# Linear attention and a GELU network on one core: a new load order and finer pieces for the first batch

## The chip, the cores and the metric

The kernel runs on one core of one Trainium2 chip. A time is the device time of one execution in microseconds. The span is what the hardware profiler shows of one execution, from the first instruction to the last; the profiled execution has a time of its own, which is a little longer than its span. All moments named below are counted from the start of the span.

## The reference

There are 8 batches, 8 heads, 576 tokens and 64 features per head. Each batch goes through a linear attention with cosine weights, and the result through a two-layer network with d_model 512 and d_ff 2048.

```python
theta = pi / 2 * pos / S                     # pos = 0 .. 575
phi(x) = concat(max(x, 0) * cos(theta), max(x, 0) * sin(theta))     # 64 -> 128 features
kv  = sum over tokens of phi(k)[f] * v[d]    # 128 x 64 for each head
z   = sum over tokens of phi(k)              # 128 for each head
att = (phi(q) @ kv) / (phi(q) . z + 1e-6)
x   = att, heads side by side                # 4608 x 512
h   = x @ w_in                               # 512 -> 2048
out = (h * sigmoid(1.702 * h)) @ w_out       # 2048 -> 512
```

Inputs and output are float32; the kernel computes its products in bfloat16 with float32 sums.

## The kernel before

One batch, 576 tokens, is one block. For each block the kernel does the following.

- `trig` (L134) and `trig_q` (L143) build phi(k) and phi(q) from the float32 tiles `kf` and `qf`. One call makes two instructions, cosine and sine. In batch 0 the nine strips j of 64 tokens are spread over VectorE and ScalarE (`act=True`).
- `kv_mm` (L197) sums phi(k) against v on TensorE, and against ones for z. `kv_evac` (L205) copies the result from PSUM to `kvs` on VectorE.
- phi(q) is turned so that features lie on partitions, in `qT`. In batch 0 TensorE does this (`qturn_pe`, L166) and VectorE or ScalarE copies it out (`qevac`, L173). In later batches SP issues transposes by DMA (`qturn_dma`, L182).
- `num_mm` (L211) multiplies 128 tokens of `qT` with `kvs`. `num_div` (L219) divides by the last column in three VectorE instructions. Its result `xn` is turned by TensorE (`xturn_mm`, L236) and copied to `x` by ScalarE (`xturn_evac`, L243) in batches 0 and 1, and by DMA (`xturn_dma`) later. Accumulators of `kv_mm`, `num_mm` and `xturn_mm` come from a PSUM pool `pat` of two buffers.
- `mm1_part` (L260) multiplies x with 128 columns of w_in, four products over the 512 features; a group `fc` is one such set of 128 hidden features, and there are 16. `gelu` (L267) applies the activation on ScalarE. The last 64 tokens of a batch go through `mm1_tail` (L278), in two halves of eight groups, with products of 64 columns (L284).
- `mm2` (L300) multiplies the activated groups with w_out for 128 tokens t at a time, in pieces lo to hi of the 16 groups. ScalarE copies the sum to `ysb`, and Pool stores it. Accumulators of `mm1`, `mm2`, `qturn_pe` and the warm-up `idle` (L314) share the PSUM pool `pmm` of four buffers.

The order of the instructions on every engine is the order in which the code is written (`tc.manual_schedule()`). Nothing is moved by a planner.

The loads go through two queues. SP issues k and q of batch 0 in two pieces each (L62, L63). Pool issues v of batch 0 into `vb` as bfloat16, w_in and w_out (cast to bfloat16 on the way), and the loads of later batches. Two of Pool's instructions are there only to make it wait: a copy of one element of `kf` into `gate` (L124), and one of `vb` (L129):

```python
nc.gpsimd.tensor_copy(gate[0:1, 0:1], kf[0:1, 0, 0:1])
for i in (0, 2):
    nc.gpsimd.dma_start(out=vb[:, i:i + 2], in_=src_of(v, 0, i, i + 2))
load_win(0, 512)
load_win(512, 1024)
nc.gpsimd.tensor_copy(gate[0:1, 1:2], vb[0:1, 3, 0:1])
load_win(1024, 1536)
load_win(1536, 2048)
```

TensorE starts with products of zeros (`idle`, L354 and L355) until phi(k) is there. `start_block` (L325) opens a batch whose x is made on TensorE: it multiplies the first four groups 128 tokens at a time, with the later numerators and turns of x between them, and then one whole group of 512 tokens. For batch 0 it runs over groups 0 to 3 and then 4; groups 5 to 15 follow whole. While batch 0 is in mm2, the kv sum and the first numerators of batch 1 are computed between its pieces, and so are the first two turns of x (L434 to L444, `opened=True`). From batch 1 on, the loop at L447 computes, during mm1 of batch b, phi(q), phi(k) and v of batch b + 1 on VectorE, and at group 15 its kv sum on TensorE. A third copy by Pool (L415) holds the loads of batch 2 until the transposes of batch 1's q have landed.

Of the kernel before, what the change touches and what calls it, by code (L numbers as in the profile page):

```python
# [9 lines left out]
F32 = mybir.dt.float32  # L10
# [9 lines left out]
def kernel(  # L20
# [9 lines left out]
    nc = tc.nc  # L30
# [21 lines left out]
    def raw(name, dt=F32):  # L52
        return one.tile([128, NI, S], dt, name=name)

    def src_of(src, b, i0=0, i1=NI):
        return src[b, 2 * i0:2 * i1].rearrange("(i hh) (p j) d -> (hh p) i (j d)", hh=2, j=NS)

    qf = one.tile([128, 2560], F32, name="qf")
    kf, vf, vb = raw("kf"), raw("vf"), raw("vb", BF16)
    qf0 = qf[:, 0:NI * S].rearrange("p (i e) -> p i e", i=NI)  # L60
    for t, src, cut in ((kf, k, 192), (qf0, q, 256)):
        nc.sync.dma_start(out=t[:, :, 0:cut], in_=src_of(src, 0)[:, :, 0:cut])  # L62
        nc.sync.dma_start(out=t[:, :, cut:S], in_=src_of(src, 0)[:, :, cut:S])  # L63


    NP = NS + 5
# [1 line left out]
    nc.gpsimd.iota(pos_i[:, 0:NS], pattern=[[1, NS]], base=0, channel_multiplier=NS)  # L68
    nc.gpsimd.iota(pos_i[:, NS:NS + 4], pattern=[[1, 4]], base=0, channel_multiplier=4)
    nc.gpsimd.iota(pos_i[:, NS + 4:NP], pattern=[[1, 1]], base=512, channel_multiplier=1)  # L70
    ident = const.tile([128, 128], BF16)
    nc.gpsimd.memset(ident, 1.0)
    nc.gpsimd.affine_select(out=ident, in_=ident, compare_op=mybir.AluOpType.is_equal,
# [22 lines left out]
    qn0 = qn.rearrange("p c h f -> p (c h f)")[:, 0:NS * NI * 128].rearrange(  # L96
        "p (j i f) -> p j i f", j=NS, i=NI)
    qT = one.tile([128, H, 640], BF16, name="qT")
    w_in_sb = one.tile([128, KC, d_ff], BF16, name="w_in_sb")
    w_out_sb = one.tile([128, FC, d_model], BF16, name="w_out_sb")  # L100
    nc.gpsimd.memset(vt[:, :, :, 64:66], 1.0)
    nc.gpsimd.memset(qT[:, :, S:640], 0.0)


    win_r = moe_w_in.rearrange("(kc p) f -> p kc f", p=128)
    wout_r = moe_w_out.rearrange("(fc p) d -> p fc d", p=128)

    def load(t, src, b):
        nc.gpsimd.dma_start(out=t, in_=src_of(src, b))
# [4 lines left out]
        nc.gpsimd.dma_start(out=qf[0:64, 2048:2560].rearrange("p (h e) -> p h e", h=H),  # L114
                            in_=q[b, :, 512:S, :].rearrange("h p d -> p h d"))

    def load_win(f0, f1):
        nc.gpsimd.dma_start(out=w_in_sb[:, :, f0:f1], in_=win_r[:, :, f0:f1])

    def load_wout(g):  # L120
        nc.gpsimd.dma_start(out=w_out_sb[:, ts(g, 4), :], in_=wout_r[:, ts(g, 4), :])

    gate = const.tile([1, 4], F32)
    nc.gpsimd.tensor_copy(gate[0:1, 0:1], kf[0:1, 0, 0:1])  # L124
    for i in (0, 2):
        nc.gpsimd.dma_start(out=vb[:, i:i + 2], in_=src_of(v, 0, i, i + 2))
    load_win(0, 512)
    load_win(512, 1024)
    nc.gpsimd.tensor_copy(gate[0:1, 1:2], vb[0:1, 3, 0:1])  # L129
    load_win(1024, 1536)  # L130
    load_win(1536, 2048)


    def trig(dst, src, j, act=False):  # L134
# [70 lines left out]
    def kv_evac(i0, i1):  # L205
        o = st["kvs"][:, :, i0:i1, 0:65]
        nc.vector.tensor_copy(o, st["ps", i0].rearrange("p hh (i e) -> p hh i e", e=65))  # L207
# [28 lines left out]
    def xturn_mm(c):  # L236
        ps, xn = nums[c]
        xv = xn.rearrange("p a h e -> p (a h e)")
        for kc in range(KC):
            o = ps[:, kc // 2, ds(264 + (kc % 2) * 64, 64)].bitcast(BF16)  # L240
            nc.tensor.transpose(o, xv[:, ts(kc, 128)], ident)  # L241

    def xturn_evac(b, c):  # L243
        ps = nums.pop(c)[0]
        n = 128 if c < 4 else 64
        i = ps[:, :, 264:392].bitcast(BF16).rearrange("p a (k t) -> p a k t", k=2)[:, :, :, 0:n]
        o = x[b][:, :, c * 128:c * 128 + n].rearrange("p (a k) t -> p a k t", a=2)
        nc.scalar.activation(o, i, AF.Copy)
# [11 lines left out]
    def mm1_part(b, fc, t0, t1):  # L260
        if t0 == 0:
            hp[fc] = pmm.tile([128, MT], F32, name="mm")
        for kc in range(KC):
            nc.tensor.matmul(hp[fc][:, t0:t1], w_in_sb[:, kc, ts(fc, 128)], x[b][:, kc, t0:t1],  # L264
                             start=(kc == 0), stop=(kc == KC - 1))

    def gelu(fc):  # L267
        g = gpool.tile([128, MT], BF16, name="g")
        nc.scalar.activation(g, hp.pop(fc), AF.Gelu_apprx_sigmoid)  # L269
        gT[fc] = g  # L270

    def mm1(b, fc):
        mm1_part(b, fc, 0, MT)
# [4 lines left out]
    def mm1_tail(b, half):  # L278
        if half == 0 and b % 2 == 0:
            gt[0] = gpool.tile([128, FC, 128], BF16, name="gtail", bufs=2)  # L280
        hps = pmm.tile([128, 8, 64], F32, name="mm")
        for f in range(8):
            for kc in range(KC):
                nc.tensor.matmul(hps[:, f], w_in_sb[:, kc, ts(half * 8 + f, 128)], x[b][:, kc, MT:S],  # L284
                                 start=(kc == 0), stop=(kc == KC - 1))
        nc.scalar.activation(gt[0][:, ts(half, 8), ts(b % 2, 64)], hps, AF.Gelu_apprx_sigmoid)  # L286

# [29 lines left out]
            nc.tensor.matmul(w[:, 0:cols], warm[:, 0:128], warm[:, 0:cols], start=True, stop=True)  # L317

    def vb_rhs(r, i, j):
        return vb[r, i, ts(j, 64)]  # L320

    def vt_rhs(r, i, j):
        return vt[r, j, i, 0:65]

    def start_block(b, opened=False):  # L325

        if not opened:
            xturn_mm(0)
            xturn_evac(b, 0)
            xturn_mm(1)  # L330
            xturn_evac(b, 1)
            num_mm(2)
            num_div(2)
        for c in range(4):
            for fc in range(4):
                mm1_part(b, fc, c * 128, c * 128 + 128)
            if c == 0:
                num_mm(3)
                num_div(3)
                xturn_mm(2)  # L340
                xturn_evac(b, 2)
            if c == 1:
                num_mm(4)
                num_div(4)
                xturn_mm(3)
                xturn_evac(b, 3)
        for fc in range(4):
            gelu(fc)
        mm1(b, 4)
        xturn_mm(4)  # L350
        xturn_evac(b, 4)


    idle(12)  # L354
    idle(100, 64)  # L355
    for j in (0, 1):
        trig(kr, kf, j)
    for j in (2, 6, 7, 8):
        trig(kr, kf, j, act=True)
    for j in (3, 4, 5):  # L360
        trig(kr, kf, j)
    kv_open(0, 2)
    kv_open(2, 4)
    kv_mm(0, NI, lambda r, i, j: ones[r, 0:1], 64, 1)
    for j in (0, 1):
        trig(qn0, qf0, j)
    qturn_pe(0)
    for j in (2, 3):
        trig(qn0, qf0, j, act=True)
    qturn_pe(1)  # L370
    idle(3)
    for j in (4, 5):
        trig(qn0, qf0, j)
    qturn_pe(2)
    for j in (6, 7):
        trig(qn0, qf0, j, act=True)
    qevac(0)
    trig(qn0, qf0, 8)
    qevac(1, act=True)
    qevac(2, act=True)  # L380
    kv_mm(0, 2, vb_rhs, 0, 64)
    kv_evac(0, 2)
    kv_mm(2, 4, vb_rhs, 0, 64)
    kv_evac(2, 4)
    qturn_pe(3)
    qevac(3, act=True)
    num_mm(0)
    num_div(0)
    num_mm(1)
    num_div(1)  # L390
    qturn_pe(4)
    qevac(4)
    x_open(0)
    start_block(0)


    load(kf, k, 1)
# [5 lines left out]
    load_wout(3)  # L403
    for j in range(NS):
        trig(kr, kf, j)
    for fc in range(5, FC):
        mm1(0, fc)
    mm1_tail(0, 0)
    mm1_tail(0, 1)
# [9 lines left out]
    for g in range(2):  # L419
        for t in range(4):  # L420
            mm2(0, t, 4 * g, 4 * g + 4)
    mm2(0, 0, 8, 12)
    mm2(0, 1, 8, 12)
    kv_open()
    kv_mm(0, 4, vt_rhs, 0, 65)
    kv_evac(0, 4)
    mm2(0, 2, 8, 12)
    mm2(0, 3, 8, 12)
    num_mm(0)
    num_div(0)  # L430
    num_mm(1)
    num_div(1)
    x_open(1)
    mm2(0, 0, 12, 16)  # L434
    mm2(0, 1, 12, 16)
    xturn_mm(0)
    xturn_evac(1, 0)
    mm2(0, 2, 12, 16)
    xturn_mm(1)
    xturn_evac(1, 1)  # L440
    num_mm(2)
    num_div(2)
    mm2(0, 3, 12, 16)
    start_block(1, opened=True)  # L444


    for b in range(1, B):  # L447
# [73 lines left out]
```

## Time and profile before

| what | value |
|---|---|
| timed runs | 295.7, 301.29, 302.06 us; median 301.29 |
| profiled execution | 295.57 us, span 293.9 us, TensorE clock 0.998 |
| TensorE busy | 283.1 us, 96% of the span |
| VectorE, ScalarE, Pool busy | 123.8, 128.0, 81.9 us |
| products with w_in (L264) | 593 seen, 113.6 us |
| products with w_out (L305) | 509 and 60 seen, 116.0 and 13.6 us |
| tail products with w_in (L284) | 512, 16.2 us |
| loads of batch 0, issue to landing | k 3.3 and 4.9, q 5.7 and 7.3, v 6.4 and 7.0 us |

A group row of the profile gives the line, the engine and the operation, the tiles it writes and reads with their shapes, how often it ran, busy time and mean duration in nanoseconds, and last the idle time of its engine just ahead of it with what ended it. In a timeline row the first two numbers are the start and the length; the brackets hold the idle time before it and what it waited for. In a row of windows there stand the window, its length, then busy time and count for TensorE's products, TensorE's weight loads, VectorE, ScalarE and Pool, the clock granted to TensorE, the share of the DMA engines and GB/s. A product's own duration contains the time through the array; in a stream the distance of the starts is what counts.

### The profile page before, as it was taken

The page shows a single profiled execution, that of the slowest core. Times are in us where ns is not written, and L with a number is a line of the kernel's source. Part 1 is how long each engine was busy: PE and PEld are TensorE (multiplying, and loading weights), DVE is VectorE, ACT ScalarE, POOL GpSimd, SP SyncE. Part 2 cuts the span into 40 slices and gives each one's busy share as a digit, 9 for nine tenths or more (in the row PEclk, how much of TensorE's full clock was granted, in tenths as well). Part 3 has the DMA queues.
Part 4 walks back from the last instruction along what each step waited for, and adds up shares of the span by engine and source line. Part 5 has one row for each costly group of instructions (what it writes and reads, how often), then busy time and mean ns, then how long its engine had stood idle before and what let it go on. Part 6 is the DMA issues. An engine that isn't in the chain of part 4 may idle for free.

```text
span 293.9 us, 6796 instructions
## 1 busy us (share of the span) xinstructions
PE 283.1 (96%) x2832; PEld 155.7 (53%) x2871; DVE 123.8 (42%) x355; ACT 128.0 (44%) x220; POOL 81.9 (28%) x96
## 2 busy tenths in 40 slices
PE   8879999999999999999999999999999999999993
PEld 4775546746544465446454465446454465445443
DVE  4674513791369125930269115950159304200000
ACT  7847642674115721465114641265114651166121
POOL 6361002635216501470215601290114300100111
PEclk9999999999999999999999999999999999999999
DMA  7999997999999876779249983889258402400112
GB/s 254 239 219 276 351 180 109 326 312 228 323 272 184 240 294 142 156 192 365 71 128 171 221 333 96 151 193 386 85 140 153 93 2 75 115 36 0 38 71 73
DMA packets 64238, 53.59 MB, mean 182 GB/s; under 512 B 49552, under 2 KB 56336, under 8 KB 64208
## 3 DMA queue, kind: packets, MB, share of 16 engines
q0 software_dynamic: 13792, 38.87, 43.3%
q1 hardware_dynamic: 50416, 14.30, 28.4%
q8 instruction: 22, 0.36, 0.5%
q14 instruction: 8, 0.07, 0.1%
HBM read 36.70 MB, written 9.44 MB: 157 GB/s over the span
## 4 chain that ended last, share of the span: by engine, by line
PE 95%; issue 1%; DVE 1%; ACT 1%; ACTq 0%
PE mm L305 42%; PE mm L264 37%; PE mm L284 5%; PE at L202 4%; PE at L215 3%; PE mm L317 3%; PE at L241 1%; DVE xn L227 1%; PE mm L170 1%; ACT g L269 1%; DVE inv L225 0%; DVE den L223 0%; ACT ysb L309 0%; DVE warm L76 0%; ACTq L269 0%
## 5 line engine op out<-in xcount | busy, mean ns | idle before, releaser
L305 PE MATMUL mm<-w_out_sb,g 128*128 128x512 bf16 (+1 forms) x509 | 116.0, 372 | 1.1 <-issue 0.2
L264 PE MATMUL mm<-xT,w_in_sb 128*128 128x512 bf16 (+1 forms) x593 | 113.6, 345 | 0.8
L312 POOL DMA_DIRECT2D out_dram<-ysb x44 | 50.7, 1152 | 169.7 <-ACT ysb L309 162.9
L269 ACT ACTIVATE g<-mm 128x512 bf16<-128x512 f32 x128 | 75.6, 598 | 39.6 <-PE mm L264 39.6
L264 PEld LDWEIGHTS <-w_in_sb 128*128 128x128 bf16 x608 | 53.8, 98 | 55.2
L305 PEld LDWEIGHTS <-g 128*128 128x128 bf16 x528 | 49.0, 98 | 50.2
L309 ACT ACTIVATE ysb<-mm 128x512 f32<-128x512 f32 (+1 forms) x37 | 21.7, 586 | 108.1 <-PE mm L305 101.9
L223 DVE TENSOR_SCALAR den<-at 128x8 f32<-128x8 f32 x40 | 6.6, 166 | 60.6 <-PE at L215 60.6
L227 DVE TENSOR_TENSOR xn<-at,inv 128x512 bf16<-128x512 f32 x40 | 27.7, 691 | 2.4 <-DMA xT<-xn 1.0
L207 DVE CAST kvs<-at 128x520 bf16<-128x520 f32 (+1 forms) x9 | 5.8, 642 | 51.3 <-PE at L202 51.2
L141 DVE TENSOR_SCALAR kr<-kf,cosw 128x256 bf16<-128x256 f32 x68 | 23.8, 350 | 6.9 <-DMA kf<-in_k_dram 6.9
L141 DVE TENSOR_SCALAR kr<-kf,sinw 128x256 bf16<-128x256 f32 x68 | 23.1, 340 | 0.0
L215 PEld LDWEIGHTS <-qT 128*128 128x128 bf16 x320 | 14.5, 97 | 7.3
L154 DVE TENSOR_SCALAR qn<-qf,cosw 128x512 bf16<-128x512 f32 (+1 forms) x33 | 15.8, 478 | 3.9 <-DMA qf<-in_q_dram 3.9
L284 PEld LDWEIGHTS <-w_in_sb 128*128 128x128 bf16 x512 | 16.0, 98 | 1.9
L284 PE MATMUL mm<-xT,w_in_sb 128*128 128x64 bf16 x512 | 16.2, 193 | 0.1
L215 PE MATMUL at<-kvs,qT 128*128 128x65 bf16 x320 | 15.9, 193 | 0.0
L154 DVE TENSOR_SCALAR qn<-qf,sinw 128x512 bf16<-128x512 f32 (+1 forms) x33 | 15.8, 479 | 0.0
L305 PE MATMUL mm<-w_out_sb,gtail 128*128 128x512 bf16 x60 | 13.6, 379 | 0.2
L202 PEld LDWEIGHTS <-kr 64*128 64x128 bf16 x648 | 10.1, 94 | 4.3 <-issue 3.7
L286 ACT ACTIVATE gtail<-mm 128x512 bf16<-128x512 f32 x16 | 9.6, 597 | 5.1 <-PE mm L284 5.1
L317 PE MATMUL mm<-warm 128*128 128x64 bf16 (+1 forms) x114 | 8.7, 240 | 1.3 <-DVE warm L76 1.3
(54 smaller groups left out, 112.0 us busy)
## 6 DMA issues: line engine op xcount, KB each, us to landing
kf<-in_k_dram POOLq DMA_DIRECT2D x7, 1152.0 KB, 9.1
vf<-in_v_dram POOLq DMA_DIRECT2D x7, 1152.0 KB, 11.8
qf<-in_q_dram POOLq DMA_DIRECT2D x7, 1024.0 KB, 7.4
out_dram<-ysb POOLq DMA_DIRECT2D x27, 256.0 KB, 2.8
out_dram<-ysb POOLq DMA_DIRECT2D x17, 128.0 KB, 7.2
w_in_sb<-in_moe_w_in_dram POOLq DMA_DIRECT2D x4, 512.0 KB, 9.7
w_out_sb<-in_moe_w_out_dram POOLq DMA_DIRECT2D x4, 512.0 KB, 18.0
qf<-in_q_dram POOLq DMA_DIRECT2D x7, 128.0 KB, 7.4
```

The costliest lines, as they stand in the source:

```text
L141: nc.vector.tensor_scalar(o, i, 0.0, w[:, j:j + 1], op0=MAX, op1=MUL)
L154: nc.vector.tensor_scalar(o, i, 0.0, sc, op0=MAX, op1=MUL)
L202: nc.tensor.matmul(st["kv", i][:, hh, ds(col, n)], kr[r, j, i, :], rhs(r, i, j), start=(j == 0), stop=(j == NS - 1))
L215: nc.tensor.matmul(ps[:, h // 4, ds((h % 4) * 65, 65)], qT[:, h, ts(c, 128)], st["kvs"][:, hh, i, 0:65], start=True, stop=True)
L227: nc.vector.tensor_tensor(xn, pv[:, :, :, 0:64], inv.unsqueeze(3).to_broadcast([128, 2, 4, 64]), op=MUL)
L264: nc.tensor.matmul(hp[fc][:, t0:t1], w_in_sb[:, kc, ts(fc, 128)], x[b][:, kc, t0:t1], start=(kc == 0), stop=(kc == KC - 1))
L269: nc.scalar.activation(g, hp.pop(fc), AF.Gelu_apprx_sigmoid)
L284: nc.tensor.matmul(hps[:, f], w_in_sb[:, kc, ts(half * 8 + f, 128)], x[b][:, kc, MT:S], start=(kc == 0), stop=(kc == KC - 1))
L305: nc.tensor.matmul(yp[t, c0][:, c0:c1], w, w_out_sb[:, fc, c0:c1], start=(fc == 0), stop=(fc == FC - 1))
L309: nc.scalar.activation(ysb[:, c0:c1], yp[t, c0][:, c0:c1], AF.Identity)
L312: eng.dma_start(out=dst[:, c0:c1], in_=ysb[p0:p0 + n, c0:c1])
L317: nc.tensor.matmul(w[:, 0:cols], warm[:, 0:128], warm[:, 0:cols], start=True, stop=True)
```

## The change

- SP's queue carries only k of batch 0. q of batch 0 goes to Pool's queue: its first 256 elements of every row (four strips), then v in two tiles `vA` and `vB`, then the rest of q, then w_in. Pool's first copy reads the cosine weights in place of `kf`, and its second one the second part of q in place of v. It stands ahead of the last part of w_in.
- w_in lies in three tiles, of 512, 512 and 1024 columns, instead of one with four loads. `wcol` picks the 128 columns of a group: every fourth column of a range of 512, instead of 128 neighbours. w_out is loaded with four neighbouring rows to a partition to match.
- Batch 0 is written out in place of `start_block(0)`. Its first eight groups are computed in halves of 256 tokens: two groups share an accumulator of 2 x 256 columns (`half_part`) and one activation (`half_gelu`). The turns of q, the numerators and the turns of x are set between them; q's strips 4 to 8 are built later than before. Groups 8 to 15 follow whole.
- The filler of zeros is 111 products of 64 columns, 16 of 128 and 6 of 512, in place of 12 of 512 and 100 of 64; a filler of three between the q turns is gone.
- For batch 1 the two first turns of x and the third numerator return to `start_block(1)`, after the last piece of mm2.

```diff
-    for t, src, cut in ((kf, k, 192), (qf0, q, 256)):
-        nc.sync.dma_start(out=t[:, :, 0:cut], in_=src_of(src, 0)[:, :, 0:cut])
-        nc.sync.dma_start(out=t[:, :, cut:S], in_=src_of(src, 0)[:, :, cut:S])
+    nc.sync.dma_start(out=kf[:, :, 0:192], in_=src_of(k, 0)[:, :, 0:192])
+    nc.sync.dma_start(out=kf[:, :, 192:S], in_=src_of(k, 0)[:, :, 192:S])
...
+    vA, vB = (one.tile([128, 2, S], BF16, name=n) for n in ("vA", "vB"))
+    w_in_t = [one.tile([128, KC, n], BF16, name=f"w_in_{i}") for i, n in enumerate((512, 512, 1024))]
+    wout_r = moe_w_out.rearrange("(g p c) d -> g p c d", p=128, c=4)
+
+    def load_win(i, f0):
+        n = w_in_t[i].shape[2]
+        nc.gpsimd.dma_start(out=w_in_t[i], in_=win_r[:, :, f0:f0 + n])
...
-    wout_r = moe_w_out.rearrange("(fc p) d -> p fc d", p=128)
...
+    def wcol(kc, fc):
+        g, c = divmod(fc, 4)
+        w = w_in_t[g][:, kc, :] if g < 2 else w_in_t[2][:, kc, ts(g - 2, 512)]
+        return w.rearrange("p (f c) -> p f c", c=4)[:, :, c]
...
-    nc.gpsimd.tensor_copy(gate[0:1, 0:1], kf[0:1, 0, 0:1])
-    for i in (0, 2):
-        nc.gpsimd.dma_start(out=vb[:, i:i + 2], in_=src_of(v, 0, i, i + 2))
-    load_win(0, 512)
-    load_win(512, 1024)
-    nc.gpsimd.tensor_copy(gate[0:1, 1:2], vb[0:1, 3, 0:1])
-    load_win(1024, 1536)
-    load_win(1536, 2048)
+    nc.gpsimd.tensor_copy(gate[0:1, 1:2], cosw[0:1, 0:1])
+    nc.gpsimd.dma_start(out=qf0[:, :, 0:256], in_=src_of(q, 0)[:, :, 0:256])
+    nc.gpsimd.dma_start(out=vA, in_=src_of(v, 0, 0, 2))
+    nc.gpsimd.dma_start(out=vB, in_=src_of(v, 0, 2, 4))
+    nc.gpsimd.dma_start(out=qf0[:, :, 256:S], in_=src_of(q, 0)[:, :, 256:S])
+    load_win(0, 0)
+    load_win(1, 512)
+    nc.gpsimd.tensor_copy(gate[0:1, 0:1], qf0[0:1, 0, 256:257])
+    load_win(2, 1024)
...
+    def half_part(fc, c0, c1):
+        pr, u, h = fc // 2, fc % 2, c0 // 2
+        if u == 0 and c0 % 2 == 0:
+            hb[pr, h] = pmm.tile([128, 2, 256], F32, name="mm")
+        t0, t1 = c0 * 128, c1 * 128
+        for kc in range(KC):
+            nc.tensor.matmul(hb[pr, h][:, u, t0 - h * 256:t1 - h * 256], wcol(kc, fc), x[0][:, kc, t0:t1],
+                             start=(kc == 0), stop=(kc == KC - 1))
+
+    def half_gelu(pr, h):
+        if h == 0:
+            gp[pr] = gpool.tile([128, 2, MT], BF16, name="gpair", bufs=4)
+            gT[2 * pr], gT[2 * pr + 1] = gp[pr][:, 0], gp[pr][:, 1]
+        nc.scalar.activation(gp[pr][:, :, ts(h, 256)], hb.pop((pr, h)), AF.Gelu_apprx_sigmoid)
...
-    idle(12)
-    idle(100, 64)
+    idle(111, 64)
+    idle(16, 128)
+    idle(6)
...
     for j in (0, 1):
         trig(qn0, qf0, j)
-    qturn_pe(0)
     for j in (2, 3):
         trig(qn0, qf0, j, act=True)
-    qturn_pe(1)
-    idle(3)
...
     kv_mm(0, 2, vb_rhs, 0, 64)
     kv_evac(0, 2)
+    qturn_pe(0)
+    qevac(0)
+    qturn_pe(1)
+    qevac(1, act=True)
     kv_mm(2, 4, vb_rhs, 0, 64)
     kv_evac(2, 4)
-    qturn_pe(3)
-    qevac(3, act=True)
     num_mm(0)
     num_div(0)
     num_mm(1)
     num_div(1)
-    qturn_pe(4)
-    qevac(4)
-    x_open(0)
-    start_block(0)
+    for j in (4, 5):
+        trig(qn0, qf0, j, act=True)
+    x_open(0)
+    xturn_mm(0)
+    xturn_evac(0, 0)
+    qturn_pe(2)
+    qevac(2)
+    xturn_mm(1)
+    xturn_evac(0, 1)
+    trig(qn0, qf0, 6)
+    trig(qn0, qf0, 7, act=True)
+    half_part(0, 0, 1)
+    half_part(1, 0, 1)
+    num_mm(2)
+    num_div(2)
+    half_part(2, 0, 1)
+    half_part(3, 0, 1)
+    trig(qn0, qf0, 8)
+    for fc in range(4):
+        half_part(fc, 1, 2)
+    half_gelu(0, 0)
+    half_gelu(1, 0)
...
-    for fc in range(5, FC):
+    for fc in range(8, FC):
         mm1(0, fc)
...
-    mm2(0, 0, 8, 12)
-    mm2(0, 1, 8, 12)
     kv_open()
     kv_mm(0, 4, vt_rhs, 0, 65)
     kv_evac(0, 4)
-    mm2(0, 2, 8, 12)
-    mm2(0, 3, 8, 12)
+    for t in range(4):
+        mm2(0, t, 8, 12)
+    x_open(1)
+    mm2(0, 0, 12, 16)
+    mm2(0, 1, 12, 16)
     num_mm(0)
     num_div(0)
     num_mm(1)
     num_div(1)
-    x_open(1)
-    mm2(0, 0, 12, 16)
-    mm2(0, 1, 12, 16)
-    xturn_mm(0)
-    xturn_evac(1, 0)
     mm2(0, 2, 12, 16)
-    xturn_mm(1)
-    xturn_evac(1, 1)
-    num_mm(2)
-    num_div(2)
     mm2(0, 3, 12, 16)
-    start_block(1, opened=True)
+    start_block(1)
```

## The prediction

> **What bounds it now.** I read the page's first parts, then TensorE's timeline, the windows, the loads' times to landing, and last the waits around the second and third batch. Times are microseconds from the start of the span unless said otherwise.
>
> ```profile
> span 293.9 us, 6796 instructions
> PE 283.1 (96%) x2832; PEld 155.7 (53%) x2871; DVE 123.8 (42%) x355; ACT 128.0 (44%) x220; POOL 81.9 (28%) x96
> PE 95%; issue 1%; DVE 1%; ACT 1%; ACTq 0%
> ```
>
> TensorE is the chain nearly everywhere. Of its 283.1 the products with zeros (group L317) are 8.7, so 274.4 is useful and no reordering can win more than 293.9 - 274.4 = 19.5. Most of that lies at the start:
>
> ```profile
> 1.26 7.99 PE L317 MATMUL mm<-warm 128*128 128x512 bf16 x112 [1.26 <-DVE warm L76]
> 9.18 1.05 PE L202 MATMUL at<-ones,kr 64*128 64x1 bf16 x72
> ...
> 13.68 1.07 PE L202 MATMUL at<-vb,kr 64*128 64x64 bf16 x60 [1.07 <-issue]
> ...
> 16.77 0.40 PE L241 MATMUL at<-ident,xn 128*128 128x128 bf16 x4 [0.76 <-DVE xn L227]
> 17.80 0.40 PE L241 MATMUL at<-ident,xn 128*128 128x128 bf16 x4 [0.64 <-DVE xn L227]
> 18.04 0.41 PE L215 MATMUL at<-kvs,qT 128*128 128x65 bf16 x8
> 18.28 1.06 PE L264 MATMUL mm<-xT,w_in_sb 128*128 128x128 bf16 x16
> ```
>
> The zeros end at 9.25; there are holes before the products with v and around the x transposes; the first product with w_in starts at 18.28. The tails (L284), which follow all sixteen groups of batch 0, start at 34.00. The loads explain the holes:
>
> ```profile
> 7.00:8.00 1.00, 1.00 (x41) 1.00 (x37) 1.00 (x5) 1.00 (x4) 0.40 (x1) 1.00 1.06 395
> 8.00:9.00 1.00, 1.00 (x41) 1.00 (x38) 1.00 (x5) 1.00 (x3) 0.00 (x0) 1.00 1.15 318
> 9.00:10.00 1.00, 1.00 (x75) 0.95 (x72) 0.59 (x3) 1.00 (x4) 0.00 (x0) 1.00 1.20 207
> ...
> 12.15 0.17 POOL L129 CAST gate<-vb 1x1 f32<-1x1 bf16 x1 [4.75 <-DMA vb<-in_v_dram]
> ```
>
> The last column is GB/s as written. Plain loads run at about 395; loads that cast to bf16 at 207 written, so about 414 read. The rate falls to 207 only after 8, so v, issued at 4.27, moved nothing until SP's k and q were nearly through, and landed at 12.1.
>
> **The loads after the change.** SP keeps k (landing 6.2). Pool's first issue no longer waits for k (copy at 4.14) but for the cosines (ACT, done 2.50), so q's first half is issued near 2.7 and queues behind k as q does now. In Pool's new order, from 6.1: q 0-255, 0.52 MB at 0.395 MB/us, lands 7.5; each half of v, 0.59 MB read at 0.41, lands 9.0 and 10.4; the rest of q, 0.66 MB, at 12.1; then the first two tiles of w_in, 1.05 MB read each (2.55), at 14.7 and 17.2, and the third, twice that, near 22.3. The total until w_in starts is what it was; v has moved ahead of half of q. Pool pays 0.75 to 0.89 for an issue (rows L118, L126) where SP paid 0.50, so its six issues end near 7.5, each before its bytes are due. Its second copy now waits for the rest of q, 12.1; queued behind it are the third tile of w_in and all loads of batch 1, whose bytes cannot move before 17.2, so that wait is covered by 5.
>
> **The first 34 us, step by step.** The zeros: 12 of 512 columns took 5.1 to about 6.3 (0.43 each), then 100 of 64 columns 29 ns each. The new filler, 111 of 64, 16 of 128, 6 of 512, at the same turning point is some 7.7 us: 9.0 in place of 9.25. kr: VectorE has four pairs after k lands instead of three, 2.02 + 0.53 = 2.55, done 8.75, against ScalarE's 8.71 now: no gain. The kv ones then run 9.0 to 10.0 (72 in 0.98). Next kv of heads 0-3, 36 at 17.8 ns (60 in 1.07), 10.65; two q transposes groups (8 at 62.5 ns, 0.5) 11.65, with the eviction of kv (0.5) and of qT (0.69) behind on VectorE; kv of heads 4-7, 12.3; its eviction 12.85; num 0 and 1 (0.24 each), 13.4; the two divisions, 1.13 and 1.05 (den 15.58 to xn end 16.71, next 17.75), 14.3 and 15.35; xT 0, q transposes 2, xT 1; first product with w_in near **15.65**, its x evicted at 15.4 and its weights landed at 14.7. That is 2.6 earlier.
>
> From there TensorE's remaining work up to the tails is, by present rows: 64 of 128 columns at 55.6 ns (16 in 0.89) 3.56; 32 of 256 columns at half of 216 ns, 3.46; 32 of 512 (43 in 9.28, 216 ns) 6.91; 12 q transposes 0.75; three num groups 0.72; three xT groups 0.72; together 16.1. Tails at **31.8** against 34.00: **-2.2**. Cover needed: groups 4-7 begin near 18.5, 1.3 after the second tile of w_in; the eight half gelus (0.60) and five x evictions (0.60) fill 7.8 of some 10 us of ScalarE. Without that cover each late microsecond is lost one for one. Bounds of this step: -3.0 if every hole goes, 0 if the loads on Pool start as late as v did.
>
> Moved out of its cover: the x transposes 0 and 1 of batch 1, now between mm2 groups (TensorE at 49.73 and 50.82, products with w_in straight on at 52.17), come after the last mm2. ScalarE then has ysb of t=3 (0.60) and the x eviction (0.60), and num 2 waits for that accumulator. TensorE has two xT groups (0.48) to set against about 1.3: 0.7, and 0.15 more before x transpose 2: **+0.85**, between +0.2 and +1.5. So batch 1 is 2.2 - 0.85 = 1.35 ahead.
>
> Load costs: load_q(1) overwrites the q tile, whose last reader moves from 12.0 to about 18; Pool now issues it at 15.95 but its bytes wait behind 2 MB of w_out and k until near 30, so nothing. Fewer, larger pieces for w_in's last tile and w_out: 0 to -0.3 on the queue, taken as -0.2. Replacing vb and w_in_sb by tiles costs no instruction.
>
> **Where the gain goes.** At batch 2's kv TensorE has no slack against VectorE:
>
> ```profile
> 49.34 0.17 POOL L415 CAST gate<-qT 1x1 f32<-1x1 bf16 x1 [25.29 <-DMA qT<-qn]
> 49.96 0.90 POOL L112 DMA_DIRECT2D qf<-in_q_dram  x1 [0.45 <-ACT ysb L309]
> ...
> 56.66 0.49 DVE L154 TENSOR_SCALAR qn<-qf,cosw 128x512 bf16<-128x512 f32 x1 [0.49 <-DMA qf<-in_q_dram]
> ...
> 65.43 1.35 DVE L162 CAST vt<-vf 128x2304 bf16<-128x2304 f32 x1
> ...
> PEld L202 <- DVE vt L162: 0.4, 1, 0.4
> ```
>
> q of batch 1 lands at 34.6 behind a full queue; its transposes by DMA share that queue and end at 49.0; Pool's copy at 49.34 lets q of batch 2 load, landing 56.6; VectorE then works without a hole (ten q halves 4.0, eighteen kr 4.7, v 1.35) until 66.78, and TensorE's kv starts at 66.88. This chain hangs on the bytes of the queue, which are unchanged, not on TensorE. A TensorE that is 1.35 early arrives at 65.5 and waits 1.1 to 1.3. Net -0.2 from the queue: span 293.7, and with the 1.67 that lie around the span in this execution (295.57 - 293.9), **295.4 us**. All steps refer to 295.57. The three timed runs are 295.7, 301.29 and 302.06; the profiled one stands with the lowest, 5.7 under their median, and no profile shows what the other two spent.
>
> **The strided weights.** wcol takes every fourth column of w_in, so every weight load of mm1 steps 8 bytes. No row before does that. Bounds: at best the same. Of the present loads, the 72 of the kv ones passed at 13.6 ns, in two halves of the array at once, so one takes at most 27; the 512 tail products run at 29.2 ns each (64 in 1.87) and hide it by 2 ns. From 29.2 on, each ns costs 512 ns in all. The nearest row, 27, doubled is 54: 512 x 24.8 = +12.7, all on TensorE, since the 128-column products at 55.6 and the longer ones still hide it. I take the low end, being the row itself; the doubled one is a rival.
>
> [...] No run here shows a stepped load.
>
> **Rivals.** (1) *The gain is kept*: the chain of batch 2 moves up with TensorE, if the transposes end earlier because w_out drains in larger pieces. For it: they share the queue until 43.7. Against: q still lands by bytes. 295.57 - 1.35 = 294.2, at the utmost 295.57 - 3.0 + 0.2 = 292.8. (2) *Slower by the strided weights*, at the tails of every batch, from 29.2 ns a load on: 295.4 + 12.7 = **308.1** at 54 ns, 303.0 at 44. For it: a margin of only 2 ns; against: nothing but that 27 is itself an upper bound. (3) *The change doesn't do what it says*: Pool's queue delivers no sooner. If its first bytes need the 4.4 that v needed (4.27 to about 8.7), q starts at 7.1 instead of 6.1 with the queue empty between; every later load, and batch 2's chain, is up to 1.0 late: 296.4. Against: v had SP's q ahead of it, the new q has only k.
>
> **Chances.** Forecast 0.47; kept 0.17; late loads 0.13; strided 0.23, of which 0.05 below 303. The range 292.8 to 303.0 leaves out 0.18; its top is a weight load of 44 ns and takes in the 302.06 of the present spread; the forecast's own range is 294.4 to 296.4. Over 2% is about what a measurement of this kernel can tell from no change: slower 0.26 (0.21 of the strided case, and 0.05 from late loads added to the spread of the runs), faster 0.07 (a kept gain beside a high run of before), same 0.67.
>
> **What would show it.** Right: first w_in product at 15 to 16.3, tails near 32, a TensorE wait of about 1 on vt ahead of batch 2's kv, and tail products still 29 ns. Wrong: tails of 64 taking 3.4 instead of 1.87 (strided), DMA idle near 6 to 7 (late loads), or kv of batch 2 at 65.5 without a wait (kept).

## The result and the profile after

The changed kernel is slower: 300.72 us in the median of six runs (297.61 to 304.62), beside 298.45 for the kernel before in the same comparison. The ratio is 1.0133, with a 95% interval of 1.0084 to 1.0183. It leaves out runs more than 1.5% above the fastest of their kernel, three of the kernel before (301.21 to 302.06) and one of the changed kernel (304.62), but not the changed kernel's at 301.68 and 301.85; lowest beside lowest is 297.61 to 295.61, or 0.7%. The change is inside 2%, and the interval lies clear of no difference. My 295.4 stood for no difference that can be measured. The profiled execution of the changed kernel is the slowest of its six (304.62), so a second one, of the same kernel at 299.24 (called "the second look" here), is read beside it.

First the head of the page, the chain's shares by engine, and the tails' two rows (busy time, mean ns of one, idle time before them). The last two lines are the same rows of the kernel before:

```profile
span 302.8 us, 6857 instructions
PE 288.5 (95%) x2868; PEld 170.2 (56%) x2905; DVE 125.2 (41%) x357; ACT 126.6 (42%) x218; POOL 83.3 (27%) x97
...
PE 88%; DMA 6%; DVE 2%; issue 1%; ACT 1%; ACTq 0%
...
L311 PEld LDWEIGHTS <-w_in 128*128 128x128 bf16 x512 | 18.4, 118 | 1.8
L311 PE MATMUL mm<-xT,w_in 128*128 128x64 bf16 x512 | 18.5, 198 | 0.0
...
L284 PEld LDWEIGHTS <-w_in_sb 128*128 128x128 bf16 x512 | 16.0, 98 | 1.9
L284 PE MATMUL mm<-xT,w_in_sb 128*128 128x64 bf16 x512 | 16.2, 193 | 0.1
```

TensorE is still the bound, but three things differ. It is busy 5.4 longer. A DMA now holds 6% of the chain. A weight load of the tails, whose weights are now every fourth column, takes 118 ns by the record instead of 98, and the 512 tail products take 18.5 us instead of 16.2. TensorE's timeline (start, duration, engine, line, operation, count, and in brackets the wait ahead of it) shows the same places as before:

```profile
9.33 1.05 PE L211 MATMUL at<-ones,kr 64*128 64x1 bf16 x72
10.24 0.42 PE L211 MATMUL at<-vA,kr 64*128 64x64 bf16 x18
...
16.24 0.61 PE L290 MATMUL mm<-xT,w_in 128*128 128x128 bf16 x8
...
32.60 2.30 PE L311 MATMUL mm<-xT,w_in 128*128 128x64 bf16 x64
34.73 7.07 PE L332 MATMUL mm<-w_out_sb,gpair 128*128 128x512 bf16 x31
...
51.67 0.40 PE L224 MATMUL at<-kvs,qT 128*128 128x65 bf16 x8 [0.48 <-ACT xT L257]
...
66.67 1.26 PE L211 MATMUL at<-vt,kr 64*128 64x65 bf16 x72
...
80.24 1.89 PE L332 MATMUL mm<-w_out_sb,g 128*128 128x512 bf16 x8
86.71 0.62 PE L224 MATMUL at<-kvs,qT 128*128 128x65 bf16 x8 [4.58 <-DMA qT<-qn]
87.14 3.60 PE L332 MATMUL mm<-w_out_sb,g 128*128 128x512 bf16 x8
```

The first product with w_in starts at 16.24 instead of 18.28, the tails at 32.60 instead of 34.00. So the start does what the change says. But 64 tails take longer. Start to start with the products that follow, they take 2.13 (32.60 to 34.73), and in the kernel before 1.86:

```profile
34.00 2.03 PE L284 MATMUL mm<-xT,w_in_sb 128*128 128x64 bf16 x64
35.86 8.80 PE L305 MATMUL mm<-w_out_sb,g 128*128 128x512 bf16 x39
```

And at 86.71 TensorE waits 4.58 for a DMA transpose of batch 2's q. Eight equal products then take 3.60, where at 80.24 they took 1.89. The windows of this execution (from 84 to 90 in steps of two; after the five engines' busy times come the granted clock, the DMA share and GB/s) show why:

```profile
84.00:86.00 2.00, 0.00 (x0) 0.00 (x0) 0.00 (x0) 0.00 (x0) 0.00 (x0) 0.85 1.15 133
86.00:88.00 2.00, 1.29 (x11) 0.74 (x12) 0.56 (x3) 0.00 (x0) 0.00 (x0) 0.50 1.28 146
88.00:90.00 2.00, 2.00 (x6) 0.73 (x5) 0.50 (x1) 0.00 (x0) 0.00 (x0) 0.50 1.10 180
```

Every engine is idle, the DMA engines are full, and after the hole TensorE's clock is 0.50. This trouble is not the change's alone: e3 below, the kernel before with one copy added, waits 2.7 for transposes of x. It has to be set aside before the change itself can be seen. The second look has no such wait, and it shows another one at the start (windows of one microsecond, 10 to 14):

```profile
10.00:11.00 1.00, 0.19 (x14) 0.10 (x7) 0.05 (x1) 0.00 (x0) 0.00 (x0) 1.00 1.16 373
11.00:12.00 1.00, 0.60 (x22) 0.55 (x22) 0.12 (x1) 0.00 (x0) 0.00 (x0) 1.00 1.01 342
12.00:13.00 1.00, 1.00 (x16) 0.83 (x12) 0.88 (x2) 0.00 (x0) 0.00 (x0) 0.72 1.21 221
13.00:14.00 1.00, 1.00 (x37) 0.97 (x36) 0.13 (x1) 0.87 (x1) 0.63 (x2) 0.50 1.24 208
```

TensorE is 0.19 and 0.60 busy, then the clock falls to 0.50 at about 12.4 and stays there until about 19.3. In the kernel before it is 1.00 in all of these windows. The tails of the second look start at 34.95, later than before. The early gain is gone there.

**The account by batches.** The starts of the eight groups of tails (one per batch) divide the span into stretches that can be compared one by one. These are the profiled executions, in us; "end" is from the last tails to the end of the span. The rows below the first three belong to the experiments.

| kernel | first tails | to batch 1 | 2 | 3 | 4 | 5 | 6 | 7 | end | span |
|---|---|---|---|---|---|---|---|---|---|---|
| before | 34.00 | 34.94 | 35.46 | 32.00 | 35.46 | 32.00 | 35.46 | 30.70 | 23.88 | 293.9 |
| after | 32.60 | 36.15 | 43.16 | 32.28 | 35.96 | 32.28 | 35.74 | 30.97 | 23.66 | 302.8 |
| after, second look | 34.95 | 36.14 | 35.74 | 32.28 | 35.74 | 32.29 | 35.74 | 30.97 | 23.65 | 297.5 |
| h3: steps, old opening | 33.27 | 35.23 | 36.84 | 32.28 | 35.74 | 32.29 | 35.74 | 30.97 | 23.64 | 296.0 |
| h4: no steps, new opening | 33.80 | 35.86 | 35.82 | 32.01 | 35.46 | 32.00 | 35.93 | 30.70 | 23.92 | 295.5 |
| h1: neither | 32.97 | 35.93 | 36.50 | 32.00 | 35.46 | 32.00 | 35.95 | 30.71 | 23.88 | 295.4 |

Against before, the second look loses 0.95 up to the first tails, 1.20 in the stretch to batch 1, 0.27 to 0.29 in each of the six that follow (1.68), and gains 0.23 at the end: 0.95 + 1.20 + 1.68 - 0.23 = 3.60, which is 297.5 - 293.9. The experiments take these terms apart.

### The profile page after: what moved, and what is told of

It reads as the page before. It is cut to its first block, busy times and chain, and to the rows that moved or that the text cites. A ratio compares the mean times of both kernels' runs of the same rounds, so it can differ in the third digit from the quotient of the medians.

```text
span 302.8 us, 6857 instructions
## 1 busy us (share of the span) xinstructions
PE 288.5 (95%) x2868; PEld 170.2 (56%) x2905; DVE 125.2 (41%) x357; ACT 126.6 (42%) x218; POOL 83.3 (27%) x97
## 4 chain that ended last, share of the span: by engine, by line
PE 88%; DMA 6%; DVE 2%; issue 1%; ACT 1%; ACTq 0%
PE mm L332 38%; PE mm L273 33%; DMA qT<-qn 6%; PE mm L311 5%; PE at L211 3%; PE at L224 3%; PE mm L344 3%; PE mm L290 2%; DVE xn L236 1%; PE at L250 1%; ACT g L278 1%; PE mm L179 0%; DVE inv L234 0%; DVE den L232 0%; ACT xT L257 0%
## 5 line engine op out<-in xcount | busy, mean ns | idle before, releaser
L332 PE MATMUL mm<-w_out_sb,g 128*128 128x512 bf16 (+1 forms) x479 | 111.4, 377 | 0.9
L273 PE MATMUL mm<-xT,w_in 128*128 128x512 bf16 (+1 forms) x514 | 106.1, 359 | 0.8
L339 POOL DMA_DIRECT2D out_dram<-ysb x44 | 52.0, 1184 | 177.4 <-ACT ysb L336 173.0
L278 ACT ACTIVATE g<-mm 128x512 bf16<-128x512 f32 x120 | 71.2, 598 | 38.6 <-PE mm L273 38.6
L273 PEld LDWEIGHTS <-w_in 128*128 128x128 bf16 x528 | 55.7, 114 | 46.2
L332 PEld LDWEIGHTS <-g 128*128 128x128 bf16 x496 | 46.6, 99 | 48.5 <-issue 2.5
L311 PEld LDWEIGHTS <-w_in 128*128 128x128 bf16 x512 | 18.4, 118 | 1.8
L311 PE MATMUL mm<-xT,w_in 128*128 128x64 bf16 x512 | 18.5, 198 | 0.0
L332 PEld LDWEIGHTS <-gtail 128*128 128x128 bf16 x64 | 6.0, 98 | 6.6
## 6 DMA issues: line engine op xcount, KB each, us to landing
vf<-in_v_dram POOLq DMA_DIRECT2D x7, 1152.0 KB, 11.6
w_in<-in_moe_w_in_dram POOLq DMA_DIRECT2D x2, 512.0 KB, 10.7
```

Source lines behind the costliest of these rows:

```text
L273: nc.tensor.matmul(hp[fc][:, t0:t1], wcol(kc, fc), x[b][:, kc, t0:t1], start=(kc == 0), stop=(kc == KC - 1))
L311: nc.tensor.matmul(hps[:, f], wcol(kc, half * 8 + f), x[b][:, kc, MT:S], start=(kc == 0), stop=(kc == KC - 1))
L332: nc.tensor.matmul(yp[t, c0][:, c0:c1], w, w_out_sb[:, fc, c0:c1], start=(fc == 0), stop=(fc == FC - 1))
L339: eng.dma_start(out=dst[:, c0:c1], in_=ysb[p0:p0 + n, c0:c1])
```

## The experiments

The theories, by the letters that the expectations use: **A**, the stepped columns slow every group of tails; **B**, holes early in batch 0 halve TensorE's clock; **C**, the DMA transposes of batch 2 land late behind the loads of batch 3; **E**, the early gain is given back at batch 2's kv. The rival to them all is that Pool's queue simply delivers no sooner.

### The stepped columns

**e2_step4**: the kernel before, with every fourth column, and w_out's rows to match:

```
-wout_r = moe_w_out.rearrange("(fc p) d -> p fc d", p=128)
+wout_r = moe_w_out.rearrange("(g p c) d -> p g c d", p=128, c=4)
 ...
+def wcol(kc, fc):
+    g, c = divmod(fc, 4)
+    return w_in_sb[:, kc, ts(g, 512)].rearrange("p (f c) -> p f c", c=4)[:, :, c]
```

> The kernel before with every fourth column to a group and w_out's rows to match, nothing else of the change. Theory A: tails at 33.3 ns, +2.1 us, lowest runs near 297.7. Rival B: as before, 295.6.

**s2_step2** and **s8_step8** are the same edit with c=2 and c=8.

> The kernel before with every second column to a group (4 bytes). If the cost grows with the distance: 29 to 31 ns for a tail product. If any step costs the same: 33 ns.

> The kernel before with every eighth column to a group (16 bytes between the columns). Read by the tail products alone; the kernel as a whole waits longer for w_in. [...] If any step costs the same: 33 ns.

The tails by groups, of e2, then s2, then s8:

```profile
L288 PEld LDWEIGHTS <-w_in_sb 128*128 128x128 bf16 x512 | 18.3, 118 | 1.6
L288 PE MATMUL mm<-xT,w_in_sb 128*128 128x64 bf16 x512 | 18.3, 198 | 0.1
```

```profile
L288 PE MATMUL mm<-xT,w_in_sb 128*128 128x64 bf16 x512 | 16.2, 193 | 0.0
```

```profile
L288 PEld LDWEIGHTS <-w_in_sb 128*128 128x128 bf16 x512 | 32.1, 167 | 1.1
L288 PE MATMUL mm<-xT,w_in_sb 128*128 128x64 bf16 x512 | 31.9, 224 | 0.0
```

The kernel before has 16.2 (its rows stand above). A step of 4 bytes costs nothing, of 8 bytes 2.1 us in 512 products (4 ns each), of 16 bytes 15.7 us (31 ns each, so 62 in place of 32). Theory A is shown alone, on the kernel before: a weight load takes 98 ns by its record in s2, as in the kernel before, 118 in e2 and 167 in s8, and the 64-column products come further apart with it. That the products then wait for the loads is inferred from these rows. The price at a step of four is small.

The times of e2 (303.66 median, 1.0266 [1.0239, 1.0293]) and of the single run of s2 (300.93) say nothing of theory A, since both hold something else, which is not in s8 (311.59, one run). The wait of e2's first product with w_in:

```profile
PE mm L268 <- DMA w_in_sb<-in_moe_w_in_dram: 4.9, 1, 4.9
```

With w_in in one tile, a stepped read of its first quarter is held until 23.35, when later parts of w_in have landed; s2 waits 4.7. That the stepped read is taken to touch the tile's other loads would be one reason. But s8 reads the same single tile with a step and starts at 18.53 without a wait, so the step in one tile is not the whole reason, and it stays open. The changed kernel, with three tiles, has no such wait. From its first tails on, e2's profile is free of this wait, and the steps, with w_out's rows to match, are its only difference from the kernel before: its seven stretches are 35.23, 35.73, 32.29, 35.73, 32.29, 35.74 and 30.96, each 0.26 to 0.29 longer than before's.

**e1_contig**: the changed kernel with 128 neighbouring columns and the old rows of w_out; its three tiles, order and halves stay:

```
-    w = w_in_t[g][:, kc, :] if g < 2 else w_in_t[2][:, kc, ts(g - 2, 512)]
-    return w.rearrange("p (f c) -> p f c", c=4)[:, :, c]
+    return w_in_t[g][:, kc, ts(c, 128)] if g < 2 else w_in_t[2][:, kc, ts(fc - 8, 128)]
```

> The changed kernel with 128 neighbouring columns of w_in to a group again (and w_out's rows as before), all else as changed. Theory A, stepped weight loads cost TensorE about 4 ns at each tail product: tails back from 33.3 to 29.2 ns each, 512 x 4.1 ns = 2.1 us off, lowest runs near 295.5 against 297.6 for the changed kernel. Rival B, the loss lies in the order of loads or in the opening of batch 1: lowest runs stay at 297.6.

299.58 (297.36 to 303.62), ratio 1.0102 [1.0053, 1.0152]: the time did not fall by more than the runs differ, which was a miss. The tails did, to 16.4. In the profiled run TensorE met two other waits:

```profile
11.65 0.74 PE L210 MATMUL at<-vA,kr 64*128 64x64 bf16 x36 [1.32 <-DMA vA<-in_v_dram]
...
86.33 0.62 PE L223 MATMUL at<-kvs,qT 128*128 128x65 bf16 x8 [3.35 <-DMA qT<-qn]
```

The first is v's first half, issued at 3.6, which lands 8.0 later here, after 6.3 in the first profile of the changed kernel. The second is theory C's. All six runs of e1 show a mean clock of 0.994 or less. A single edit could not be read as long as B and C moved more than 2 us from run to run.

### Late transposes in batch 2

**e3_gate_before** and **e4_gate_after** give the kernel before and the changed kernel one more copy on Pool ahead of the load of the next q, so that this load starts only when the last transpose of the present q has landed:

```
+nc.gpsimd.tensor_copy(gate[0:1, 3:4], qT[0:1, 7, S - 1:S])
 # ahead of load_q(nb + 1)
```

> The kernel before, and in the batch loop Pool waits, with a copy of one element of qT, for the last DMA transpose of the next batch's q ahead of that loop pass's loads. Theory C, the runs near 301 are those in which the loads of batch 3 get into the DMA queue ahead of the last transposes of batch 2, so that TensorE waits some 5 us for them and then runs 3 us at half clock: all runs between 295.2 and 296.5. Rival D, the high runs come from the chip's state: about half the runs still at 301 to 302.

> The changed kernel with the same wait of Pool. Theory C: all runs between 297.2 and 298.3. Rival D: a spread from 297.6 to 304 as without it.

e3: 299.22 (296.86 to 302.58), ratio 1.0087 [1.0053, 1.0121], slower than without it, and the spread stays. The wait moved:

```profile
PE mm L264 <- DMA xT<-xn: 2.7, 1, 2.7
```

The transposes that come late are now the next ones, those of x. So theory C holds as a description (a transpose that lands late, while large loads run, stops TensorE), but the copy does not cure it; that the later load is what holds them was not tried by itself. e4: 299.08, five of six between 298.81 and 299.19, ratio 1.0101 [1.008, 1.0123]. There the spread nearly goes, with no wait for qT in its profile, and the level stays 3 us above before. That level is not theory C. Its profile has the half clock from 11.6 to 15.0, and tails at 34.53.

**a2_after** is the changed kernel once more, the second look of above.

> The changed kernel once more, on the chip of the three below. Theory C (late transposes of batch 2 in some executions): a spread from about 297.6 to 302. Profile: tails at 33.3 ns.

298.80 (298.06 to 302.12), ratio 1.0107 [1.0057, 1.0157], with mean clocks of 0.986 to 0.994 in all six runs.

### Moving the second kv, and undoing the opening, with the half clock still there

**e5_contig_gate** is e1 with the gate. **e6_kvlate** adds to it that batch 2's kv runs after the tails of batch 1:

```
-            if nb is not None and fc == 15:
+            if nb is not None and fc == 15 and b != 1:
 ...
+        if b == 1:
+            kv_open(); kv_mm(0, 4, vt_rhs, 0, 65); kv_evac(0, 4)
```

**e7_opened** adds to e6 the old opening of batch 1, with the x transposes 0 and 1 among the mm2 groups.

> The changed kernel with neighbouring columns and with Pool's wait for the transposes. Theories A and C together: 2.1 us under the changed kernel's undisturbed runs, 295.5 to 297, with a spread under 1 us. Rival (the two do not add): like the one with neighbouring columns alone, 297.4 to 301.

> As the one before, and batch 2's kv products on TensorE moved from ahead of group 15 of batch 1 to behind its tails, where VectorE's v is ready. Theory E, what TensorE wins at the start is given back at those products: 0.5 to 1.3 us under the one without the move. Rival F, there is no gain left to give back after the opening of batch 1: within 0.3 us of it.

> As the one before, and batch 1 opened as in the kernel before (first two turns of x and third numerator between the last pieces of mm2). My estimate of the cost of the new opening, 0.85 us: another 0.6 to 1.0 us less. If the opening costs nothing: no change.

e5: 303.41, ratio 1.0207 [1.0145, 1.0269], with a wait of 2.0 for v, the half clock, and 1.8 for the transposes of x. e6: 298.94, ratio 1.011 [1.007, 1.0151]. e7: 303.85, ratio 1.0251 [1.0209, 1.0292], with its profile's row:

```profile
PE mm L272 <- DMA xT<-xn: 6.4, 1, 6.4
```

All three miss what was expected. In the profiles e5 waits 1.8 for transposes, e6 not at all, e7 6.4, and all three have the half clock, so they say nothing clean on E or on the opening; both had to be read without it.

### Filling the early holes

**g1_fill**: the changed kernel with ten more products with zeros, in the two holes of batch 0:

```
 # after the kv ones
+idle(6)
 # ahead of the first x transposes
+idle(4)
```

> The changed kernel with ten more products of zeros of 512 columns on TensorE: six behind the ones of kv and four ahead of the first turn of x. They compute nothing that is used. Theory B, TensorE's holes near 10 to 15 us halve its clock for 3.4 to 6.8 us in most executions: with the holes filled there is no half-clock window ahead of 80 us, mean clock 0.996 or more, lowest runs 297 and most within 298. Rival H, the half clock comes whatever is done there, or costs nothing since TensorE waits anyway: 298 to 300 as without, or 1 us more for the products added.

298.27; four of the six runs are 297.76 to 298.42, at mean clocks of 0.998 to 1.000; ratio 1.0075 [1.0059, 1.0091]. The profiled execution is its slowest (303.68), with waits of 0.8 and 3.0 for transposes of batch 2, so only its start is read here. Its windows, as those of the second look:

```profile
10.00:11.00 1.00, 1.00 (x7) 0.32 (x7) 0.00 (x0) 0.00 (x0) 0.00 (x0) 1.00 1.14 342
11.00:12.00 1.00, 0.94 (x40) 0.79 (x40) 0.03 (x1) 0.00 (x0) 0.00 (x0) 1.00 1.03 373
12.00:13.00 1.00, 1.00 (x26) 0.90 (x26) 0.88 (x2) 0.04 (x1) 0.00 (x0) 1.00 1.20 219
13.00:14.00 1.00, 0.79 (x40) 0.65 (x35) 0.60 (x2) 1.00 (x2) 0.93 (x3) 1.00 1.24 207
```

Theory B is shown for the clock: with products that compute nothing it is 1.00 at the start of all six profiles with the filler, and it falls to 0.50 there in five of the seven without. The tails start at 33.22 instead of 34.95. A hole does not always halve the clock. In these windows of e1, with less work than in the second look, it stays at 1.00:

```profile
10.00:11.00 1.00, 0.33 (x28) 0.26 (x21) 0.00 (x0) 0.00 (x0) 0.00 (x0) 1.00 1.10 361
11.00:12.00 1.00, 0.35 (x22) 0.35 (x23) 0.00 (x0) 0.00 (x0) 0.00 (x0) 1.00 1.01 327
```

The half-clock stretches at the start last 3.4 (four profiles) or 6.8 (the second look). What sets these lengths is not shown, nor how long or how empty a hole must be. Between the first filler and these stretches the longest wait of TensorE goes from 0.32 (e7) to 1.96 (e5), while the 1.32 of e1 were followed by none, and in e7 TensorE was 0.52, 0.85 and 0.78 busy in the three microseconds from 8 to 11. In time B is worth about 0.3%, 1 us, and the two intervals overlap, so its worth is not shown. It leaves 0.75%.

**g2_fill_contig_kvlate** has g1's filler, the neighbouring columns, and the late kv.

> The same, with neighbouring columns for each group and batch 2's kv products behind the tails of batch 1, and without the wait of Pool. Theories A, B and E together: 2.1 under the one above and 0.5 to 1 more, near 294.5 in undisturbed runs, 1 us better than the kernel before. If the start stays as late as in the executions seen so far: 296 to 298.

297.49, ratio 1.0055 [1.002, 1.009]. Its profile has the clock at 1.00 at the start and a span of 295.3. Its kv starts at 11.57, right behind six products of the filler (v's first half, issued at 3.6, had landed 6.1 later), and its tails at 33.94. The stretch to batch 1 takes 34.56 without batch 2's kv and the next one, with it, 37.23; their sum is 1.39 over before's. In h4 below, the same kernel with the kv in its place, the sum is 71.68, 0.11 less. Moving the kv won nothing, so theory E in the form "kv in the wrong place" fell.

### Steps and opening, with the clock held

Four kernels with g1's filler, beside g1: **h1_fill_contig_opened** has neither steps nor the new opening, **h3_fill_step4_opened** has the steps, **h4_fill_contig** has the new opening. **h2_q_on_sp** is h1 with q's first half back on SyncE's queue, behind k. The edits are those of e1, e7 and g1; that of h2:

```
 nc.sync.dma_start(out=kf[:, :, 192:S], in_=src_of(k, 0)[:, :, 192:S])
+nc.sync.dma_start(out=qf0[:, :, 0:256], in_=src_of(q, 0)[:, :, 0:256])
 ...
-nc.gpsimd.dma_start(out=qf0[:, :, 0:256], in_=src_of(q, 0)[:, :, 0:256])
```

> The changed kernel with three parts taken back or mended: neighbouring columns to a group, the old opening of batch 1, and the ten products of zeros in the holes. Left of the change are the order of the loads, the three tiles of w_in and batch 0 in halves. If these win what remains of the start: 294.5 to 295.5, up to 1 us better than before. If v's late landing eats it: 295.5 to 296.5, the same as before.

> As the one above, with the first half of batch 0's q back on SP's queue behind k, so that Pool's queue begins with v. If it is Pool's queue that makes v late: v's first half lands at 9 to 9.5 and the time is 0.5 to 1 us under the one above. If v waits for the bytes ahead of it in either queue: no difference.

> As the first of these, with the change's every fourth column and its layout of w_out. Theory A: 2.2 us more than the first. Rival, w_out's larger pieces give some of it back on the queue: 1 to 1.8.

> As the first of these, with the change's opening of batch 1. My estimate: 0.85 us more than the first, its first product of batch 1 with w_in some 19.0 behind the start of batch 0's tails instead of 18.2. If the wait for v of batch 2 levels it out: less than 0.3.

| ratio to before, filled | old opening | new opening |
|---|---|---|
| neighbouring columns | h1 1.0013 [0.9975, 1.0051] | h4 1.0023 [0.9991, 1.0054] |
| every fourth column | h3 1.0026 [1.0004, 1.0048] | g1 1.0075 [1.0059, 1.0091] |

Without the two, what is left (the order of the loads, three tiles, halves) can't be told from the kernel before; with both it is 0.75% slower. The difference of the corners is 0.62% or 1.8 us. But g1 ran beside other executions of the kernel before than the three others, with a mean 0.8 lower; the means behind the ratios are 298.10 for g1 and 297.08 for h1, so by the times alone it is 1.0. How it divides is not shown by the times. Each alone comes to 0.1%, inside the intervals, where 2.2 us were expected for h3 and 0.85 for h4: a miss for h3, and for h4 the case of less than 0.3.

The table of stretches divides it. With steps, the stretches to batches 2 to 7 of the second look are 0.27 to 0.29 longer than before's, as e2's are, and so are h3's from batch 3 on. With the one to batch 1 (36.14 against 35.86 of h4) seven stretches give 1.96. The end is 0.23 shorter, so 1.7 in all; it holds the tails of batch 7 too, but from the issue of the last store to the end of the span it is 3.55 in the second look and 3.64 in e2 instead of 4.04, and why stays open. The opening is 35.86 of h4 against 34.94 of before: 0.92. The first product of batch 1 with w_in stands 19.04 behind the start of batch 0's tails in h4, as expected, and 18.17 in the kernel before. Neither h1 nor h3 turns its missing opening into time, and the stretches to batches 1 and 2 show why. Rows of the timelines there, h1, then h2, then h3:

```profile
42.13 1.89 PE L331 MATMUL mm<-w_out_sb,g 128*128 128x512 bf16 x8 [0.22 <-DMA w_out_sb<-in_moe_w_out_dram]
...
66.84 1.26 PE L210 MATMUL at<-vt,kr 64*128 64x65 bf16 x72 [0.54 <-DVE vt L170]
...
82.89 0.42 PE L223 MATMUL at<-kvs,qT 128*128 128x65 bf16 x8 [0.86 <-DMA qT<-qn]
```

```profile
81.78 0.42 PE L223 MATMUL at<-kvs,qT 128*128 128x65 bf16 x8 [0.94 <-DMA qT<-qn]
```

```profile
90.21 5.13 PE L273 MATMUL mm<-xT,w_in 128*128 128x512 bf16 x23 [0.93 <-DMA xT<-xn]
```

In h1 the first tails begin 1.03 earlier than before. TensorE then stands 0.22 for w_out, 0.54 for VectorE's v, so that batch 2's kv starts at 66.84 where the kernel before had 66.88, and 0.86 for the transposes of q. h2 and h3 stand 0.94 and 0.93 for transposes. The first three columns of the table, added, give the start of batch 2's tails: 104.40 before, 105.40 in h1, 105.34 in h3 (0.56 of it the steps), 105.48 in h4 (0.92 of it the opening); for h2 it is 104.29, from stretches of 32.77, 34.95 and 36.57. None is ahead of before by then by more than 0.11, though all but h4 began 0.7 to 1.2 ahead. This is theory E in its wider form, in one profile of each: what is early at the start is given back by the tails of batch 2, to work that waits for DMA, at the transposes more than at kv. That it must be so in every execution is not shown. The 0.5 in the stretch to batch 6, in h1, h2 and h4 alike, holds an "issue" wait of 0.31 to 0.34 within the tails; what sets it was not looked into.

h2 came to 297.32, ratio 1.0007 [0.9974, 1.004], span 294.2. It is no better than h1 in any measurable way. v's first half landed at 10.4 there, not at 9 to 9.5, so no gain from taking q's first half off Pool's queue was measured. No version that ran beats the kernel before, so none is proposed.

## Why the prediction was wrong

**The strided weights: the step that failed.** "I take the low end, being the row itself" put their cost at +0. The runs show 4 ns for each of the 512 tails: 2.1 us in e2, where only they and w_out's rows to match are present, and 1.7 over the span. The mechanism was that of rival 2, at a sixth of its 12.7. The row I leaned on, at most 27 ns for a weight load, left a margin of 2 ns, and it was a row of neighbouring columns, which bounds nothing for a step. With a margin that thin even a few ns more are paid in full by all eight batches, and they outweigh a gain that is made once.

**The loads, mis-sized, and the hole misread.** "Each half of v ... lands 9.0 and 10.4". In the profiles with the new order v's first half lands between 9.7 and 11.7, in the first one at 9.9, the second half at 11.3. The bytes came later than the rate of the queue gave. In the kernel before the halves landed at 10.7 and 12.1, so v came 1.0 sooner at best and 1.0 later at worst, and the rival that Pool's queue delivers no sooner held in part. "The loads explain the holes" was too simple as well: the row it rests on, at 13.68, says 1.07 "issue", with v landed at 12.1. In five of the seven profiles of the new order without filler TensorE waits 0.3 to 2.0 for v. In the second look v's first half had landed by 9.7, and TensorE stopped for 1.21 between two products with it:

```profile
11.40 0.45 PE L211 MATMUL at<-vA,kr 64*128 64x64 bf16 x18 [1.21 <-issue]
```

What TensorE waits for there, the profile does not show. The consequence that I did not name is the clock: with little to do between the kv ones and v, it halves for 3.4 to 6.8 in five of the seven. I had counted the holes as time lost or won, and not as a condition for the clock.

**The early gain: right in kind, mis-sized.** First product with w_in at 16.24 (15.65 predicted), tails at 32.60 (31.8), so -1.4 where I had -2.2, in one execution; +0.95 in the second look. With the filler and the clock at 1.00 the tails start at 32.77 to 33.94, so -0.1 to -1.2. The wider bounds that I gave, -3.0 to 0, did not hold a clock at half speed.

**The new opening: right.** +0.85 predicted, 0.92 measured between h4 and before. The sum as I wrote it was off by a tenth: 1.3 less 0.48 is 0.8 and not 0.7, which gives 0.95.

**The gain is given back: right in the sum, not in the place.** I named VectorE's v ahead of batch 2's kv with a wait of 1.1 to 1.3, since v would be ready at 66.78 whatever TensorE did. Only h1 shows such a wait, of 0.54. In h2 and h3 v is ready at 65.33 and 65.95, and the kv starts at 65.65 and 66.42 without a wait: there the chain had moved up with TensorE, as in rival 1. The gain was lost 16 to 24 later, with 0.9 at the transposes of q or x. I had also put these transposes on the queue of the loads. They are issued by SP, the loads by Pool, and the profile lists two queues; the time of both is counted there on the same 16 DMA engines, 43.3% and 28.4% of their span in the kernel before.

**w_out in larger pieces: not seen.** The -0.2 has no trace in any stretch up to the last tails.

**The sum.** By the measured terms the changed kernel without half clock or late transposes should have a span of 293.9 - 1.4 (early) + 0.9 (opening) + 1.7 (steps) = 295.1, or 296.2 with the 1.0 to 1.1 that h1 and h2 lost in the stretch to batch 2. The span of its lowest run, 295.8, lies between the two. Its two profiled runs add late transposes (the first) and the half clock (the second look); the others have no profile. Why the transposes are late in one run and not in the next stays open. No edit here controlled it: the gate moved the wait in e3, and what sets the order in which a small transpose and a large load are served was not isolated.

## What to carry over

A cost that is hidden by an estimated margin of 2 ns may not be hidden (here it was 4 ns for each of 512 tails, 2.1 us): price it at a few ns and multiply by all batches before a gain made once in the first batch is weighed against it. When work at the start is moved forward, look at the holes that it leaves in TensorE as well as at their length, since in five of the seven profiles without filler the clock stood at 0.50 for 3.4 to 6.8 us after such holes, and with ten products of zeros it was 1.00 there in all six. Before a gain is counted, find the next places that are fed by DMA; an engine that arrives earlier there may wait for the same bytes, as TensorE did for 0.86 to 0.94 us at the transposes in h1, h2 and h3.

## What the runs showed of the hardware

Behind products of 64 columns, a weight load whose columns step by 4 bytes costs the same as with neighbours (16.2 us for 512 tails in s2 and in the kernel before); by 8 bytes 512 tails take 18.3 us (e2), by 16 bytes 31.9 (s8). The same load of v, issued at 3.6 in each case, landed after 6.0 to 8.1 in twelve executions. TensorE waited up to 6.4 us (e7) for transposes by DMA that came late. In the second look two microseconds with TensorE 0.19 and 0.60 busy went ahead of a clock of 0.50 for 6.8 us, in e1 two with 0.33 and 0.35 did not, and with ten products of zeros it was 1.00 at the start of all six profiles.
